# A gated recurrence with a convolution behind it: convolution sums in PSUM, q loaded one token to a partition, paired normalizers, and a new order of all steps

## The chip, the cores and the metric

The kernel runs on one core of a Trainium2 chip. The metric is the device time of one execution in microseconds (us). The core's engines are PE (matrix multiplication), DVE and ACT (elementwise work from SBUF or PSUM), POOL (elementwise work in SBUF), and SP, which here only issues DMAs. Every engine works through its own instructions in the order in which they were issued, and waits where one needs another engine's result.

## What is computed

Inputs are fp32: q, k, v, o_gate of shape (4, 8, 768, 40), i_gate and f_gate (4, 8, 768), w_val and w_out (320, 320), conv_w (5, 320).

```python
for t in range(S):                                   # mLSTM, per batch and head
    m_new  = max(f[t] + m, i[t])
    C = exp(f[t] + m - m_new) * C + exp(i[t] - m_new) * outer(v[t], k[t])
    n = exp(f[t] + m - m_new) * n + exp(i[t] - m_new) * k[t]
    y[t] = sigmoid(o[t]) * (C @ q[t]) / max(abs(n @ q[t]), 1)
x    = y as (B, S, H * D)                            # 320 columns
gate = sigmoid(sum_k conv_w[k] * x[t - 4 + k])       # causal, 5 taps
out  = (gate * (x @ w_val)) @ w_out
```

## The kernel before, in words

The sequence is cut into 6 tiles j of 128 tokens; tile j and batch b make unit u = 4j + b, and each unit's two halves of 64 tokens make the groups g = 2u + p, 48 in all. Within a group all 8 heads are worked at once in chunked form: a matrix of decays between the tokens of the half, a score matrix, and a carried state of 40 x 41 per head (the 41st column is n).

All work is a list of small steps in the string `PLAN`; a loop at the end calls each step's function in that order. `probs.7=V` runs probs for group 7 on DVE; V, A, P and S are DVE, ACT, POOL and SP's DMA queue. `args.2#5` is a PE step that writes PSUM bank 5. There are eight banks of 512 fp32 per partition. So the order on each engine is the order of its steps in `PLAN`, buffers are taken in rotation, and a step waits until its buffer or bank is free.

Steps that the change or the prediction speaks of, with their lines before:

- Loads: ldq (L404, L407) brings q. In tile 0 a partition holds one token; in later tiles the 128 partitions are four batches of 32, each with four tokens in a row (runs of 640 bytes). ldk, ldv, ldo bring k, v and the output gate; cpk (L416) copies k to the layout `kp` that the state needs, mostly as a DMA.
- Operands: mx and scs (L488, L502 to L507) find a power of two as scale for each token, hi (L534 to L538) and lo (L543) split q and k into fp16 parts in `stk`; then either a DMA transpose (trd, L555) or PE transposes and a copy out of PSUM (trp L560, trc L564) turn them.
- Since the scale of q lies four tokens to a partition, smul (L517), sout (L522) and sctc (L526) bring it to one token a partition by a small matmul.
- Group steps: args (L576, the exponents of the decays), expo (L580), scores (L593), probs (L598, score times decay into `pk`), keyw (L606, the weighted keys), then heads (L633, numerators and normalizer), state (L616, the carried state) or both in one (both, L642), and stout (L625, state back to SBUF).
- Unit steps: norm (L648 absolute value, L651 to L655 maximum with the scale, L657 reciprocal), rsm (L661, the output gate divided by the normalizer), gate (L664, x), xeh and xel (a split of x's last 64 columns), xtr (L686, PE transposes of x), xcc, xhc, x3c and xlo (the transposed x and its parts).
- Tile steps, the feed-forward part: cv0 (L722, the first tap, POOL) and cv (L728, four taps on DVE, each adding to `gt` in SBUF) for the first two column blocks of 128, cv3 (L748, L750, PE) for the third of 64, g3c, sigm (L761), val (L771), zmul (L776), zhi and zlo (a split), outp (L793), obc (L797), od (L800).
- Gate tables: sig_ and sia bring the gates' running sums into `la` and `ra`, the operands of args, one DMA for tile 0 and one for all other tiles; cla copies the constant part with a DMA of 600 KB.

Of the kernel before, what the change touches and what calls it, by code (L numbers as in the profile page):

```python
# [29 lines left out]
raj.1=A lo.0.0.0=V ldo.0=S scs.0.0.2.3.4.0=V mx.1.1.0=A trp.0.0.0#0 gates.1.7=V trp.0.1.1#1 trc.0.0.0=A  # L30
scs.0.0.2.1.2.3=V lo.0.1.0=V mx.0.2.0=A lo.0.0.1=V trp.0.1.0#2 scs.0.0.2.3.4.1=V trc.0.1.1=A trp.0.0.1#3
scs.0.0.2.3.4.3=V laj=V scs.0.0.2.2.3.0=V sia.0.0=S scs.0.0.2.0.1.3=V mx.1.0.0=A trc.0.1.0=V sig_.0=S mx.1.3.1=A
scs.0.0.2.2.3.1=V scs.0.0.2.2.3.3=V hi.0.2.1=P selb=V wcv.5.5=A wld.0.0=S wcv.5.3=V sia.0.1=A gates.1.8=V mx.1.1.1=A
ldv.0.0=S trc.0.0.1=V hi.0.3.0=A wld.1.0=S hi.0.2.0=V scores.1#4 mx.1.0.1=A gates.1.9=V sct0=A args.2#5 wcv.5.4=V
lo.0.2.1=V args.0#6 cpk.0.1.1=S scs.0.0.2.1.2.2=V trp.0.2.1#7 zcmp.1.1=V scs.0.0.2.0.1.2=V cpk.0.0.1=S sigo.0=A
wcv.0.0=V hi.0.3.1=V ldv.0.1=S scores.0#0 lo.0.3.0=V raj.3=V trp.0.3.0#1 wcv.0.1=V wcv.5.6=V scs.1.1.2.0.4.0=V
lo.0.2.0=V expo.0=A scs.1.1.2.0.4.1=V scs.1.0.1.0.4.0=V trp.0.2.0#2 lo.0.3.1=V wcv.0.5=A keyw.0=P args.1#3 probs.0=V
chh=A raj.5=A hi.1.0.1=V cdd.0.1=A both.0#6 expo.1=A wcv.0.2=V ldk.2.2.4=S scs.1.0.1.0.4.1=V gates.1.10=V trc.0.2.0=A
wcv.0.3=V ldq.2.0=S idk1.1=V trc.0.2.1=A args.4#0 wcv.0.4=P trp.0.3.1#3 probs.1=V wld.1.1=S args.7#2 idk0.1=A expo.2=A
args.3#7 wcv.0.6=V scores.3#4 ldk.2.0.2=S gates.1.11=V stout.0=A keyw.2=P scores.2#5 ldq.2.1=S hi.1.1.0=A heads.1#6  # L40
trc.0.3.1=V hi.1.0.0=A probs.2=V keyw.1=P hi.1.1.1=A lo.1.0.0=V both.2#3 soa.1.3=S whi.0.0=A scs.0.0.2.3.4.2=V
scs.0.0.2.2.3.2=V lo.1.1.0=V expo.3=A ldq.2.3=S norm.0.0=V lo.1.0.1=V state.1#5 wld.2.0=S stout.2=A norm.0.1=V
probs.3=V trc.0.3.0=A sog.1=S args.5#7 keyw.3=P wcv.1.0=V ldq.2.2=S args.6#4 expo.5=A trp.1.0.0#1 norm.0.2=V wld.2.1=S
wcv.1.1=V rsm.0=P expo.4=A scores.4#7 raj.4=V soa.1.2=S hi.1.2.0=A heads.3#3 keyw.4=P probs.4=V cpk.1.1.0=S expo.6=A
cdd.0.0=P gate.0=V cla.0=S scores.6#0 smul.1=P norm.1.0=A expo.7=A wcv.1.2=V wlo.0.0=P scores.7#7 norm.1.1=V
trc.1.0.0=V raj.2=A sout.1#4 soa.1.0=S trp.1.1.0#6 lo.1.1.1=V sctc.1=A mx.2.2.1=A zxc=P both.4#2 wcv.1.3=V sig_.1=S
trc.1.1.0=A norm.1.2=V wcv.1.4=P rsm.1=V soa.1.1=S mx.2.0.0=A trp.1.0.1#1 hi.1.3.0=P probs.6=V stout.4=A scores.5#4
cdd.0.4=A wcv.2.0=V xeh.0=P state.3#6 mx.2.0.1=A probs.5=V cdd.0.3=P cla.1=S open_late=X xel.0=P mx.2.2.0=A zx3=V
stout.1=V heads.5#2 mx.2.1.1=A keyw.6=V wcv.2.1=V mx.2.3.0=A both.6#0 lo.1.2.0=V wcv.2.5=A hi.1.2.1=V mx.2.1.0=A
scs.1.1.2.0.4.3=V trc.1.0.1=A gate.1=V trp.1.2.0#4 wcv.2.2=V trp.1.1.1#5 scs.2.0.1.0.4.0=V zcmp.1.0=V probs.7=V  # L50
stout.6=A xtr.0#3 sia.1.0=S scs.2.0.1.0.4.1=V norm.2.0=A keyw.5=V trc.1.2.0=A heads.7#0 cpk.1.0.0=S hi.1.3.1=V
ldv.1.0=S state.5#1 norm.2.1=V xeh.1=A lo.1.2.1=V mx.2.3.1=A lo.1.3.0=V norm.3.0=A stout.5=A norm.2.2=V trp.1.3.0#7
wcv.1.5=A rsm.2=P xhc.0=A trc.1.1.1=A trc.1.3.0=V ovc.1.0=P xel.1=P gate.2=V xtr.1#4 cdd.0.2=A sia.1.1=S wcv.2.3=V
args.10#1 x3c.1=A scs.2.1.2.0.4.0=V ldv.1.1=S scores.10#7 norm.3.1=V x3b.5=A scs.1.1.2.0.4.2=V stout.3=A wcv.1.6=V
# [892 lines left out]
```

## Time and profile before

| what | value |
|---|---|
| median of 3 runs | 249.64 us (248.62 to 251.87) |
| the profiled execution | 249.69 us |
| its span in the profile | 247.9 us |
| mean granted TensorE clock | 0.985 |
| DVE / PE / ACT / POOL busy | 221.7 / 210.1 / 171.3 / 119.6 us |

The profile is one execution. Its span runs from the first to the last instruction; the 1.8 us around it are launch and end. "Busy" counts an engine's instructions, not its waits. The ends of pipelined matmuls are modelled, so neighbouring PE rows overlap; from the start of one row to the start of the next is what it really took. A buffer's number is left out in the names, and `bank` stands for all eight PSUM banks.

### The profile page before, as it was taken

How to read it: one execution, taken by the hardware profiler on the slowest of the kernel's cores; microseconds unless marked ns; L12 is line 12 of the kernel's file. 1: busy time of each engine (PE TensorE's matmuls, PEld its weight loads, DVE VectorE, ACT ScalarE, POOL GpSimd, SP SyncE). 2: the span in 40 equal slices, each digit the busy share in tenths (PEclk: the TensorE clock that was granted, in tenths of full speed). 3: DMA queues.
4: the chain of work that ended last, by engine and by line, in shares of the span. 5: the costliest groups of instructions: out<-in, count | busy, mean ns of one | idle time of the engine just before them, and what ended most of it. 6: DMA issues, size and time to landing. Idle time of an engine off the chain costs nothing.

```text
span 247.9 us, 5992 instructions
## 1 busy us (share of the span) xinstructions
PE 210.1 (85%) x2141; PEld 180.4 (73%) x2141; DVE 221.7 (89%) x523; ACT 171.3 (69%) x395; POOL 119.6 (48%) x187
## 2 busy tenths in 40 slices
...
GB/s 137 151 121 157 154 154 202 201 168 146 150 150 193 155 170 170 176 222 161 175 171 189 216 195 184 169 208 162 140 95 149 71 71 1 0 82 54 79 108 106
DMA packets 130228, 35.72 MB, mean 144 GB/s; under 512 B 118310, under 2 KB 128086, under 8 KB 130198
## 3 DMA queue, kind: packets, MB, share of 16 engines
...
## 4 chain that ended last, share of the span: by engine, by line
PE 29%; DVE 26%; DMA 14%; ACT 10%; issue 8%; POOL 7%; SPq 3%; ACTq 0%; POOLq 0%; DVEq 0%
PE bank L642 7%; DMA sg<-in_o_gate_dram 5%; PE bank L633 5%; DVE sg L728 4%; PE bank L793 4%; DVE stk L543 3%; PE bank L771 3%; DMA out_dram<-ob 3%; ACT sg L761 2%; ACT junk L488 2%; DMA tq<-stk 2%; DVE pk L598 2%; DVE sg L776 2%; PE bank L593 2%; PE bank L560 2%
## 5 line engine op out<-in xcount | busy, mean ns | idle before, releaser
L642 PE MATMUL bank<-vc,pk 128*104 128x41 f32 x384 | 41.3, 270 | 1.7 <-DVE pk L606 1.0
L642 PEld LDWEIGHTS bank<-vc,pk 128*104 128x104 f32 x384 | 38.8, 178 | 3.8 <-DVE pk L606 1.1
L728 DVE SCALAR_TENSOR_TENSOR sg<-xc,cwt,sg 128x512 f32<-128x512 f32 (+1 forms) x56 | 40.2, 732 | 0.2
L598 DVE SCALAR_TENSOR_TENSOR pk<-bank,cmp,dm 128x512 f32<-128x512 f32 x48 | 35.4, 740 | 3.3 <-PE bank L593 2.4
L580 ACT ACTIVATE dm<-bank 128x512 f32<-128x512 f32 x48 | 28.3, 596 | 12.4 <-PE bank L576 5.0
L606 POOL TENSOR_TENSOR pk<-kp,dm 128x320 f32<-128x320 f32 (+1 forms) x27 | 22.8, 849 | 21.5 <-ACT dm L580 9.1
L593 PE MATMUL bank<-tq,tk 120*128 120x64 f16 x384 | 27.7, 243 | 5.8 <-DVE tk L564 3.2
L560 PE MATMUL bank<-idh,stk 128*120 128x128 f16 x128 | 13.7, 280 | 21.1 <-DVE stk L543 20.8
L593 PEld LDWEIGHTS <-tk 120*128 120x128 f16 x384 | 23.2, 122 | 11.3 <-issue 6.8
L633 PEld LDWEIGHTS bank<-vc,pk 104*64 104x64 f32 x384 | 24.6, 140 | 8.7 <-issue 2.7
L633 PE MATMUL bank<-vc,pk 104*64 104x41 f32 x384 | 27.4, 233 | 3.2 <-ACT vc L625 1.3
L543 DVE SCALAR_TENSOR_TENSOR stk<-nat,scl,stk 128x320 f16<-128x320 f32 x48 | 28.8, 605 | 1.5 <-POOL stk L538 1.3
L560 PEld LDWEIGHTS <-stk 128*120 128x120 f16 x128 | 12.5, 187 | 23.1 <-DVE stk L543 22.1
L534 ACT ACTIVATE stk<-nat,scl 128x640 f16<-128x640 f32 x27 | 21.8, 827 | 8.2 <-DVE scl L504 3.7
L661 POOL TENSOR_TENSOR rs<-sg,den 128x320 f32<-128x320 f32 x16 | 12.6, 788 | 29.6 <-DVE den L657 29.5
L488 ACT ACTIVATE junk<-nat 128x320 bf16<-128x320 f32 x48 | 22.5, 469 | 4.7 <-DMA nat<-in_q_dram 3.0
L625 ACT COPY vc<-bank 40x328 f32<-40x328 f32 x36 | 15.3, 424 | 13.1 <-PE bank L642 10.9
L793 PE MATMUL bank<-woh,zh 128*128 128x320 f32 x72 | 19.6, 328 | 0.5 <-DVE x L707 0.4
L711 POOL TENSOR_TENSOR xl<-xc,xh 128x256 fp32r<-128x256 f32 x18 | 15.3, 853 | 8.5 <-ACT xh L699 6.3
L576 PE MATMUL bank<-ra,la 120*128 120x512 bf16 x48 | 19.3, 427 | 0.0
L793 PE MATMUL bank<-wol,zh 128*128 128x320 f32 x72 | 18.3, 309 | 0.0
L538 POOL TENSOR_SCALAR stk<-nat,scl 128x640 f16<-128x640 f32 x10 | 8.8, 882 | 19.7 <-ACT junk L488 9.5
...
## 6 DMA issues: line engine op xcount, KB each, us to landing
nat<-in_q_dram SPq DMA_DIRECT2D x24, 160.0 KB, 3.9
...
vc<-in_v_dram SPq DMA_DIRECT2D x12, 320.0 KB, 6.5
out_dram<-ob SPq DMA_DIRECT2D x24, 160.0 KB, 1.8
kp<-nat SPq DMA_DIRECT2D x22, 160.0 KB, 3.1
nat<-in_k_dram SPq DMA_DIRECT2D x10, 320.0 KB
...
raw<-in_moe_w_val_dram SPq DMA_DIRECT2D x5, 160.0 KB, 3.1
```

The source lines that it names most:

```text
L488: A.activation(junk, part(j, x, i), AF.Abs, accum_out=amx[j % 2][:, x, i : i + 1])
L534: A.activation(o, s, AF.Copy, scale=f)
L543: V.scalar_tensor_tensor(t[:, :, c : c + D], part(j, x, i), scl[j % 2][:, x, i : i + 1], t[:, :, 0:D], op0=ALU.mult, op1=ALU.subtract,)
L560: nc.tensor.transpose(t[0:K3, h], stk[(j * B + i) % NSTK][:, x, h, 0:K3], id16)
L580: A.activation(dms[g % NDM], late["psd", g], AF.Exp)
L593: nc.tensor.matmul(o, tk[h], tq[:, h], start=True, stop=True)
L598: V.scalar_tensor_tensor(pks[g % NPK][:, :, 0:L], late["pss", g], cmp_[j % 2][:, p, b : b + 1], dms[g % NDM], op0=ALU.mult, op1=ALU.mult,)
L606: eng[e].tensor_mul(pks[g % NPK][0:n, :, L:], kp[0:n, p, b * H : (b + 1) * H], dms[g % NDM][0:n, :, L - 1 : L].to_broadcast([n, H, D]),)
L633: nc.tensor.matmul(ph[p * L : (p + 1) * L, h], pks[g % NPK][0:n, h, 0:L], vc[j % 2][0:n, p, b * H + h], start=True, stop=True,)
L642: nc.tensor.matmul(ph[0 : L + D, h], pks[g % NPK][:, h], vc[j % 2][:, p, b * H + h], start=True, stop=True)
L728: V.scalar_tensor_tensor(o, xc[j % 2][:, c, b0:b1, t : t + P], cwt[:, c, t : t + 1], o, op0=ALU.mult, op1=ALU.add)
L793: nc.tensor.matmul(po, z, w, start=(i == 0), stop=(i == len(mm) - 1))
```

## The change

The functions change as follows (helpers that are no longer called are left out):

```diff
-    NTK, NTQ, NSTK, NDM, NPK, NX, NRS, NOB, NDEN, NXE = 3, 2, 2, 3, 2, 2, 2, 2, 3, 2
+    NTK, NTQ, NSTK, NDM, NPK, NX, NRS, NOB, NDEN, NXE = 3, 2, 3, 3, 3, 3, 3, 2, 3, 3
+    SL = 2
-    la = cst.tile([KA, 2, NJ, B, P], BF16, name="la")
+    la = cst.tile([KA, 2, SL, B, P], BF16, name="la")
...
     def ldq(e, j, b):
...
-        if j == 0:
-            hs = slice(b * H, (b + 1) * H)
-            dma(e)(nat[0][:, 0, hs], qv[ts, hs])
-            return
-        dst = nat[j % 2][:, 0].rearrange("p (h r) d -> p h (r d)", r=R)
-        dma(e)(dst[b * PB : (b + 1) * PB], q[b, :, ts].rearrange("h (g r) d -> g h (r d)", r=R))
+        hs = slice(b * H, (b + 1) * H)
+        dma(e)(nat[j % 2][:, 0, hs], qv[ts, hs])
...
+    def sig_(e, j):
+        src = gdg[min(j, 1)].rearrange("x p b h j t -> (x p b) h j t")
+        dma(e)(ra[L : L + NGR, :, j % SL], src[:, :, max(j - 1, 0)])
...
+    def warm(b_, i):
+        for _ in range(8):
+            nc.tensor.matmul(bank(b_, H, L), tl[:, 0, 0], tr, start=True, stop=True)
...
     def norm(e, u, s):
...
-        elif s == 0:
-            V.tensor_scalar(d, nq, -1.0, sct[j % 2][:, b : b + 1], op0=ALU.mult, op1=ALU.max)
-        elif s == 1 and ("na", u) in late:
-            V.tensor_scalar_max(d, d, sct[j % 2][:, b : b + 1])
+        d = dens[u // 2 % NDEN]
+        if s == 0:
+            A.activation(d[:, u % 2], late["ph", u][:, :, D:DT], AF.Abs)
         elif s == 1:
-            V.tensor_tensor(d, nq, d, op=ALU.max)
+            c = scl[j % 2][:, 0, b : b + 2, None, None].to_broadcast([P, 2, H, 1])
+            eng[e].tensor_tensor(d, d, c, op=ALU.max)
...
-            xi = xf[:, c * P : (c + 1) * P] if c < 2 else xes[u % NXE].bitcast(F32)
-            nc.tensor.transpose(px[:, c], xi, ident)
+            if c < 2:
+                nc.tensor.transpose(px[:, c], xf[:, c * P : (c + 1) * P], ident)
+            else:
+                nc.tensor.transpose(px[:, c].bitcast(F32R), xes[u % NXE], idr)
```

`PLAN` is new from the first step to the last. One line of its convolution, before and now:

```diff
-norm.5.2=V trd.2.2.0=S wcv.3.0=V keyw.15=P probs.15=V args.20#6 keyw.16=P stout.14=V sigo.1=A ldv.2.0=S whi.2.3=V
-heads.15#3 cv0.0.1.0.4=P norm.4.2=V ldv.2.1=S hi.2.2.1=A state.15#5 rsm.5=V rsm.4=V stout.13=A cpk.2.1.0=S lo.2.2.1=V
+expo.36=A probs.35=V heads.33#4 stout.34=A gate.14=V state.33#3 cva.2.0.0.4#2 lo.4.3.1=V heads.34#6 x3c.13=A keyw.35=V
+trd.4.3.1=S expo.37=A keyw.36=P cvp.2.0.1.0.4=V cva.2.1.0.4#5 state.35#7 cpk.4.1.1=P cvp.2.0.2.0.4=V heads.35#6
```

In counts of steps, before and after:

| step | before | after |
|---|---|---|
| first tap | 14 cv0 on POOL | 14 cva on ACT, into a PSUM bank |
| taps 2 to 5 | 56 cv on DVE, sums in SBUF | 56 cvp on DVE, sums in the bank, the fifth tap's result to SBUF |
| norm on DVE | 24 + 10 + 24, one unit each | 12 + 12, two units each |
| norm on ACT (absolute value) | 14 | 24 |
| smul / sout / sctc / selb, selg, sct0 | 5 / 5 / 5 / 3 | none |
| both / heads / state | 24 / 24 / 20 | 0 / 48 / 44 |
| cpk | 22 DMAs, 2 DVE | 2 DMAs, 2 DVE, 9 ACT, 11 POOL |
| cla / sig_ / sia | 2 / 2 / 4 DMAs | 0 / 6 / 12, each tile's own |
| warm (8 args-shaped matmuls, result unused) | 0 | 3 |
| hi: DVE, ACT, POOL | 11, 27, 10 | 5, 24, 19 |
| keyw: DVE, POOL | 17, 27 | 10, 34 |
| rsm: DVE, POOL | 8, 16 | 4, 20 |
| trc: DVE, ACT | 5, 11 | 10, 6 |
| xlo: DVE, POOL | 6, 18 | 11, 13 |
| zhi: DVE, ACT | 4, 17 | 10, 11 |
| scs (scales of q and k): DVE | 46 | 36 |

On DVE, the first column block's convolution of tile 0 before: `sg` holds the sums, and the taps (L728) stand between a state copy (L625), probs (L598), the low parts of the operands (L543) and single normalizers (L653, L657).

```order
L625 COPY vc1_82<-bank0_68 40x328
L543 SCALAR_TENSOR_TENSOR stk1_113<-nat0_78,scl0_108,stk1_113 128x8x40
L728 SCALAR_TENSOR_TENSOR sg_83<-xc0_86,cwt_95,sg_83 128x512
L598 SCALAR_TENSOR_TENSOR pk0_118<-bank7_75,cmp1_102,dm2_117 128x8x64
L543 SCALAR_TENSOR_TENSOR stk0_112<-nat0_78,scl0_108,stk0_112 128x8x40
L728 SCALAR_TENSOR_TENSOR sg_83<-xc0_86,cwt_95,sg_83 128x512
L653 TENSOR_SCALAR den1_121<-den1_121,sct1_104 128x8
L657 RECIPROCAL den2_122<-den2_122 128x8
L829 TENSOR_SCALAR wa_151<-raw1_148 128x320
L598 SCALAR_TENSOR_TENSOR pk1_119<-bank5_73,cmp1_102,dm0_115 128x8x64
```

Now, on DVE at tile 0's convolution; the first rows are the second column block's sum in bank 2, `bank5` is the first block's, L622 is the step gate, L613 a paired maximum.

```order
L700 SCALAR_TENSOR_TENSOR bank2_70<-xc0_87,cwt_96,bank2_70 128x512
L663 COPY xc1_88<-bank3_71 128x2x128
L700 SCALAR_TENSOR_TENSOR bank2_70<-xc0_87,cwt_96,bank2_70 128x512
L480 TENSOR_SCALAR amx1_107<-amx1_107 128x8
L482 TENSOR_SCALAR scl1_105<-amx1_107 128x8
L622 TENSOR_TENSOR x1_125<-bank5_73,rs1_122 128x320
L700 SCALAR_TENSOR_TENSOR bank2_70<-xc0_87,cwt_96,bank2_70 128x512
L506 SCALAR_TENSOR_TENSOR stk1_109<-nat1_80,scl1_105,stk1_109 128x8x40
L700 SCALAR_TENSOR_TENSOR bank5_73<-xc0_87,cwt_96,bank5_73 128x512
L613 TENSOR_TENSOR den1_119<-den1_119,scl0_104 128x16
L700 SCALAR_TENSOR_TENSOR sg_84<-xc0_87,cwt_96,bank2_70 128x512
```

The sum of a block moved from SBUF to a bank until its last tap, the taps of the two blocks stand among each other, and the normalizer's row has 16 columns.

On PE in tile 0 before: scores of group 5 (L593), state of group 3 (L616), heads of group 5 (L633), the fused step of group 6 (L642), then transposes for tile 1 (L560).

```order
L593 LDWEIGHTS tk2_98
L593 MATMUL bank4_72<-tq0_99,tk2_98 128x64
L616 MATMUL bank6_74<-vc0_81,pk1_119 40x41 x8
L633 MATMUL bank2_70<-vc0_81,pk1_119 64x41 x8
L642 MATMUL bank0_68<-vc0_81,pk0_118 104x41 x8
L560 LDWEIGHTS stk0_112
L560 MATMUL bank4_72<-idh_77,stk0_112 120x128
```

Now, on PE in tile 1, heads (L595) and state (L578) of groups 11 to 14, with an args matmul (L543) between.

```order
L595 MATMUL bank0_68<-vc1_83,pk2_117 64x41 x8
L578 MATMUL bank2_70<-vc1_83,pk2_117 40x41 x8
L595 MATMUL bank1_69<-vc1_83,pk0_115 64x41 x8
L543 LDWEIGHTS la_85
L543 MATMUL bank7_75<-ra_86,la_85 128x512
L578 MATMUL bank4_72<-vc1_83,pk0_115 40x41 x8
L578 MATMUL bank2_70<-vc1_83,pk2_117 40x41 x8
L595 MATMUL bank5_73<-vc1_83,pk2_117 64x41 x8
L578 MATMUL bank4_72<-vc1_83,pk1_116 40x41 x8
L595 MATMUL bank1_69<-vc1_83,pk1_116 64x41 x8
```

The fused step is gone; heads and state of a group follow one another or stand some steps apart, each writing a bank of its own.

## Rows read from the trace of the kernel before

**Rows 1.** The profile's page: busy time, share of the span and instructions of each engine; and, from its fourth part, the chain of work that ended last, by engine.

```profile
PE 210.1 (85%) x2141; PEld 180.4 (73%) x2141; DVE 221.7 (89%) x523; ACT 171.3 (69%) x395; POOL 119.6 (48%) x187
...
PE 29%; DVE 26%; DMA 14%; ACT 10%; issue 8%; POOL 7%; SPq 3%; ACTq 0%; POOLq 0%; DVEq 0%
```

**Rows 2.** Busy time of each engine in five stretches of the span. [...]

```profile
0.00:20.00 20.00, 0.00 (x0) 0.00 (x0) 16.69 (x43) 10.66 (x22) 11.61 (x31) 1.00 0.86 135
20.00:57.80 37.80, 32.09 (x356) 28.20 (x356) 34.54 (x92) 33.91 (x80) 13.25 (x19) 0.95 0.96 173
57.80:181.40 123.60, 114.90 (x1254) 96.19 (x1251) 114.47 (x269) 96.75 (x221) 66.66 (x99) 0.99 1.18 175
181.40:226.40 45.00, 44.95 (x403) 38.44 (x403) 40.07 (x89) 20.96 (x51) 22.09 (x30) 1.00 0.33 67
226.40:247.90 21.50, 18.14 (x135) 17.55 (x133) 15.95 (x34) 9.02 (x23) 5.97 (x9) 0.99 0.25 85
```

**Rows 3.** The timeline of PE, its last row. Columns: start us, us, engine, line, operation, out<-in, shapes, count.

```profile
244.23 0.31 PE L793 MATMUL bank<-wol,zh 128*128 128x320 f32 x1
```

**Rows 4.** The timeline of PE at places where it works without a gap (L576 args, L593 scores, L633 heads, L616 state, L642 the fused step, L686 transposes of x, L771 val). Columns as above; `[idle before <-releaser]` at a row's end where PE waited.

```profile
76.37 0.81 PE L616 MATMUL bank<-vc,pk 104*40 104x41 f32 x16
77.12 0.62 PE L593 MATMUL bank<-tq,tk 120*128 120x64 f16 x8
...
193.81 1.13 PE L633 MATMUL bank<-vc,pk 104*64 104x41 f32 x16
194.87 1.66 PE L642 MATMUL bank<-vc,pk 128*104 128x41 f32 x16
196.35 0.39 PE L576 MATMUL bank<-ra,la 120*128 120x512 bf16 x1
196.58 0.38 PE L686 MATMUL bank<-ident,x 128*128 128x128 f32 x2
...
198.29 1.52 PE L593 MATMUL bank<-tq,tk 120*128 120x64 f16 x24
199.62 0.83 PE L576 MATMUL bank<-ra,la 120*128 120x512 bf16 x2
200.38 0.95 PE L633 MATMUL bank<-vc,pk 104*64 104x41 f32 x13
...
201.84 1.66 PE L642 MATMUL bank<-vc,pk 128*104 128x41 f32 x16
...
203.61 0.71 PE L771 MATMUL bank<-xh,wvh 128*128 128x512 f32 x2
...
205.55 0.45 PE L793 MATMUL bank<-woh,zh 128*128 128x320 f32 x2
```

**Rows 5.** Groups of PE instructions by line from 57.8 to 181.4 us. Columns: line, engine, operation, out<-in, shapes, count | busy us, mean ns of one | idle time before them and what ended it.

```profile
L642 PE MATMUL bank<-vc,pk 128*104 128x41 f32 x256 | 26.3, 263 | 1.7 <-DVE pk L606 1.0 <-DVE x L664 0.3 <-ACT den L648 0.2
L593 PE MATMUL bank<-tq,tk 120*128 120x64 f16 x248 | 19.0, 249 | 2.2 <-DMA tk<-stk 1.5 <-DVE pk L598 0.4 <-ACT tk L564 0.4
L633 PE MATMUL bank<-vc,pk 104*64 104x41 f32 x240 | 17.2, 234 | 2.2 <-ACT vc L625 1.3 <-DVE vc L625 0.8
L576 PE MATMUL bank<-ra,la 120*128 120x512 bf16 x34 | 13.0, 400 | 0.0
L616 PE MATMUL bank<-vc,pk 104*40 104x41 f32 x243 | 12.9, 208 | 0.9 <-DVE pk L598 0.5 <-DVE den L657 0.4
```

**Rows 6.** Groups of DVE instructions by line and shape, whole span. Columns as in the group above.

```profile
L598 DVE SCALAR_TENSOR_TENSOR pk<-bank,cmp,dm 128x512 f32<-128x512 f32 x48 | 35.4, 740 | 3.3 <-PE bank L593 2.4 <-PE bank L642 0.4 <-ACT dm L580 0.4
L728 DVE SCALAR_TENSOR_TENSOR sg<-xc,cwt,sg 128x512 f32<-128x512 f32 x40 | 32.0, 807 | 0.1
...
L776 DVE TENSOR_TENSOR sg<-bank,sg 128x512 f32<-128x512 f32 x10 | 6.8, 685 | 0.8 <-PE bank L771 0.7
...
L657 DVE RECIPROCAL den<-den 128x8 f32<-128x8 f32 x24 | 4.7, 197 | 0.3
L699 DVE CAST xh<-bank 128x256 fp32r<-128x256 f32 x11 | 4.6, 415 | 0.1
L661 DVE TENSOR_TENSOR rs<-sg,den 128x320 f32<-128x320 f32 x8 | 3.9, 500 | 0.2
...
L653 DVE TENSOR_SCALAR den<-den,sct 128x8 f32<-128x8 f32 x14 | 3.9, 276 | 0.7 <-ACT den L648 0.7
...
L858 DVE CAST wvh<-wf 128x256 fp32r<-128x256 f32 x1 | 0.3, 278 | 0.0
```

**Rows 7.** The instructions of two lines, probs (L598) and the convolution taps (L728). Columns: line, engine, operation, names, count: shortest/median/longest in ns, first and last start in us; shapes.

```profile
L598 DVE SCALAR_TENSOR_TENSOR pk<-bank,cmp,dm x48: 692/740/753, 32.3 to 213.9; 128x512 f32<-128x512 f32 x48
...
L728 DVE SCALAR_TENSOR_TENSOR sg<-xc,cwt,sg x56: 469/743/1284, 77.9 to 238.3; 128x512 f32<-128x512 f32 x40, 128x256 f32<-128x256 f32 x16
```

**Rows 8.** DMA: the packets of the span by size; and the issues by out<-in, with queue, operation, count, KB of each, median us from issue to landing.

```profile
DMA packets 130228, 35.72 MB, mean 144 GB/s; under 512 B 118310, under 2 KB 128086, under 8 KB 130198
...
nat<-in_q_dram SPq DMA_DIRECT2D x24, 160.0 KB, 3.9
...
vc<-in_v_dram SPq DMA_DIRECT2D x12, 320.0 KB, 6.5
```

**Rows 9.** Groups of instructions from the page's fifth part: the exp on ACT and the subtraction xlo on POOL.

```profile
L580 ACT ACTIVATE dm<-bank 128x512 f32<-128x512 f32 x48 | 28.3, 596 | 12.4 <-PE bank L576 5.0
...
L711 POOL TENSOR_TENSOR xl<-xc,xh 128x256 fp32r<-128x256 f32 x18 | 15.3, 853 | 8.5 <-ACT xh L699 6.3
```

More of the change, by code (lines that the diff above doesn't have):

```diff
@@ L30 @@
[L30 to L54, printed above, removed]
```

337 lines of the change are left out of this document (161 added, 176 removed).

## The prediction

> **What bounds the kernel now.** I read the page's busy line first: DVE 89%, PE 85%, ACT 69%, POOL 48%, and a chain that changes engine all the time (PE 29%, DVE 26%, DMA 14%) [rows 1]. An average of two engines near 90% decides nothing, so next come the busy times by stage, cut where the program changes character [rows 2]. Until 57.8 us (last heads matmuls of tile 0) the program fills: PE does not start before 20 us, DVE is busy 16.7 of 20.0 and then 34.5 of 37.8 us. From 57.8 to 181.4 us tiles overlap: PE 114.9 and DVE 114.5 of 123.6 us. From 181.4 to 226.4 us PE is full (44.95 of 45.0). The rest is the tail; the last matmul ends at 244.5 us, 3.4 us before the span's end [rows 3]. So three limits follow one another: DVE with its feeders at the start, a tie in the middle, PE alone at the end. DVE time saved at the end is worth nothing.
>
> How much PE loses in the middle is read from dense pitches, start to start, since modelled ends overlap [rows 4]: an args matmul 0.23 us (196.35 to 196.58), eight scores 0.44 (1.33 for 24), heads and state side by side 1.46 (200.38 to 201.84), the fused step 1.49 (194.87 to 196.35), a val step of eight 1.94. Times the counts of that stage ([rows 5], 16 records a step for heads, state and the fused one, 8 for scores): fused 16 x 1.49 = 23.8; heads with state 15 x 1.46 = 22, up to 27 where they stand apart (heads alone 1.06, from 193.81 to 194.87, state alone 0.75, from 76.37 to 77.12); scores 31 x 0.44 = 13.6; args 34 x 0.23 = 7.8; from the order, nine val steps (66 matmuls) x 0.24 = 16; eight outp of eight matmuls of 320 columns, 5/8 of val's, x 1.2 = 9.7; three third-block convolutions of ten matmuls x 0.24 = 7.2; transposes about 6. Together 106 to 111, say 108. Of 123.6 us, 15.6 are lost: 8.7 shown idle, about 1.2 from the granted clock of 0.99, the rest as stretched records. That is all a faster DVE can give back in the middle.
>
> **The change part by part.** Durations are those of the profiled execution: 249.69 us, a span of 247.9 and 1.8 around it; the median of the runs is 249.64, so no correction.
>
> *DVE* [rows 6]. Normalizers: before 14 x 276 and 24 x 197 ns, and 20 more rows of about 0.19 = 12.3 us; after 12 maxima and 12 reciprocals of 16 columns. No row has 16 columns: from the same as for 8 (197) to double; at 200 each, 4.8 us: -7.5. Key and query scales of eight columns instead of twice four: ten rows fewer of that small size, at 0.23: -2.3. Selection helpers gone, five at most 0.3: about -1.3. To other engines: hi 6, keyw 7, rsm 4; from them: trc 5, xlo 5, zhi 6. All are of 250 to 1000 columns and near the row of rs, 0.5: 17 x 0.5 out, 16 x 0.5 in, -0.5. Small casts, fills, weight splits and gate steps: some fifteen rows fewer at about 0.5: -8.
>
> *Convolution.* All 56 taps stay on DVE, now from and into a PSUM bank; POOL's first tap becomes 14 ACT copies. No row has the new form. The nearest is the probs product, same instruction, 128x512, one operand from PSUM, 740 ns, with 692 to 753 over 48 [rows 6, 7], while the taps take 807 at that size and scatter from 469 to 1284 [rows 7]. Taken at 740: 56 x 67 ns = -3.8. Lower bound: zmul, a product with PSUM of that size, 685, gives 56 x 122 = -7. Upper: a cast that reads PSUM takes 415 against 278 from SBUF; if the 42 taps that write PSUM paid these 137 ns for it, +5.8, less the 3.8, is +2.
>
> [...]
>
> The sum for DVE is -23.4 us of rows. Neighbouring records overlap (all groups of that view add up to some 253 us against 221.7 busy), so about -20 of busy time: 221.7 to some 201.
>
> *ACT and POOL* [rows 9]. ACT: +14 copies for the first taps and +9 key copies, all near the 0.6 of an exp, and +10 small absolute values, against three hi, five trc (about 1.0 each) and six zhi: +14.8 less 11, +4 on 171.3. POOL: +11 key copies, +9 hi, +7 keyw, +4 rsm, less 14 first taps, five xlo, four scale products: 8 rows net, at the 0.85 of an xlo row +7 on 119.6, and to +17 with fills, gate and weight steps put there: 52 to 56% of the span. Both are hidden as long as a key copy is done before its tile's first keyw, else each costs its own 0.6 to 0.9 us in front of a state step: POOL is busy 66.7 of 123.6 us in the middle, ACT 96.8 [rows 2].
>
> *DMA.* Twenty copies of keys (160 KB each) and two copies of tables leave the queue. q in 160-byte runs instead of 640 adds packets; those of tile 0 go that way already, and v, in the same runs, lands in 6.5 us for 320 KB, against 3.9 for q's 160 KB [rows 8]: q lands 0 to 2.6 us later. It is issued a tile ahead: no cost. [...] The gate tables refilled by tile (sig_, sia) wait on SP until the tile two before has done its last args; behind them stand operand transposes and output stores. I cost that at nothing, since each refill stands a tile ahead of its use; if it is wrong, scores wait for the transposes, some us a tile, which is case (a).
>
> *PE.* Heads alone take 1.06, state alone 0.75, the two side by side 1.46, so 0.35 is saved where they are neighbours that write different halves of the partitions. Before: 24 x 1.49 + 24 x 1.06 + 20 x 0.75, less 16 such neighbours x 0.35 = 70.6. After: 48 x 1.06 + 44 x 0.75 - 41 x 0.35 = 69.5. So -1, and +13 if none of them saved anything, which the row of 200.38 excludes for most. Five scale matmuls go: -0.3. The warm packs are 24 matmuls of the args shape at 0.23 to twice that at half the clock: +5.5 to +11. The first pack stands in PE's waits at the start, the other two (3.7 to 7.4) after the eleventh and twelfth args, in tile 1: with the savings +4 in the middle. They may lift the clock of the start (0.95 until 57.8 us [rows 2], about 1.9 us lost); not counted.
>
> **The sum along the path.** Start: DVE steps up to the eighth probs shrink by about 5 us (in rows: hi -2, gates -3, norm -3, gate -2, trc +3), but ACT's list up to the eighth exp grows by as much; I take half: 57.8 - 3 = 54.8. Middle: 108 work + 4 added + 8 of the 15.6 lost, since DVE's 20 us of relief and a third buffer for probs, x and stacked operands remove waits on DVE but not those on DMA and clock = 120. End: 63.1 from 181.4 to 244.5, PE-full, unchanged, and 3.4. Together 241.3 of span, + 1.8 = 243.1 us.
>
> **The rivals.** (a) Nothing gained in the middle: PE work is the bound, the lost 15.6 us come from the order (waits on transposes and evictions) and come back elsewhere. For it: in the rows of the middle no releaser of PE has more than 1.5 us, and DVE is only one of them [rows 5]. 54.8 + 123.6 + 4 + 66.5 = 248.9 of span, 250.7 us. (b) Slower: the sums hold banks. Each of 14 sums sits in one of eight banks from ACT's copy to the fourth tap; four taps at 0.74 with other DVE rows between them are 5 to 6 us, two at a time in places, and PE, in order, stands before any matmul planned for that bank. It decides once a hold delays PE by 0.8 us on average (14 x 0.8 over 243.1 passes 254.6): at 1 us each it is 257 us. For it: in the order PE has only one to five steps between the place of the last tap and the next matmul into that bank, never more than two sums at once. Against it: the last tap goes to SBUF and ends the hold, and at a PE step of 0.4 to 2 us two steps cover a tap that is two places late. (c) Much faster: PE loses 5 in the middle and the start follows DVE entirely: 51.8 + 113 + 66.5 = 231.3, 233 us. (d) Dear taps: writing a bank costs what reading one costs a cast, the upper bound above; DVE saves 15 instead of 20, the start regains 2 and the middle 6: 55.8 + 122 + 66.5 + 1.8 = 246 us.
>
> **How the numbers follow.** About 2% (244.6 and 254.6 us) is what a measurement of this kernel can tell from no change. Forecast 0.42, (c) and steps towards it 0.1, (d) 0.13, (a) 0.22, (b) 0.13. Faster by over 2%: most of the forecast and (c), together 0.50; slower: (b) and the far side of (a), 0.16; within: 0.34. Range 232 to 255: from (c) through (a), the far part of (b) left out. The likeliest alone: 239 to 247.
>
> **What would show it.** Right: the tap row in PSUM near 740 ns with a narrow spread; normalizer rows of some 200 ns, 24 in all; DVE busy near 201 us; PE's stage from tile 1 to the fifth tile's first heads shorter by about 4 us and as full as now in the last 60; POOL below 60%. Wrong: taps above 800 ns (d); PE idle with a convolution tap as releaser (b); PE idle in the middle traced to POOL's keyw or key copies; or heads and state, apart, taking over 1.6 together in the full stretches.

## The result

The changed kernel took 234.65 us (median of 4 runs, 231.87 to 242.1) against 250.75 us for the kernel before on the same chips (248.62 to 253.71): a ratio of 0.931, 95% interval 0.914 to 0.949 (the ratio is that of each kernel's fast executions, within 1.5% of its fastest; the two medians give 0.936). Forecast were 243.1 us, a range of 232 to 255, and 0.50 for faster. The direction was right and the time lies in the range, but the gain is about two and a half times the forecast one.

One thing is needed to read every number below: executions of the same kernel differ by stretches of 3 to 27 us in which PE's granted clock is 0.5 of the full one, and so a time means little without the mean clock beside it. The profile taken with the result had such stretches:

```profile
PEclk9999999558999959589999999999999999999999
```

Its mean clock was 0.943 and it took 242.1 us; eight transposes of `stk` took 0.88 us in it at half clock (46.26 to 47.14) and 0.45 at the full one (58.95 to 59.40). The other three executions had 0.978 to 0.984 and 231.87 to 235.36 us. So the lines below are from a second profile of the same kernel, 229.73 us at 0.993 (run e1_after). Its page:

```profile
span 227.9 us, 6769 instructions
...
PE 196.6 (86%) x2544; PEld 168.5 (74%) x2544; DVE 204.1 (90%) x448; ACT 177.6 (78%) x413; POOL 127.6 (56%) x216
...
PEclk9999999999999889999999999999999999999999
```

Against [rows 1]: DVE 204.1 us (forecast 201), PE 196.6 (before 210.1), POOL 56% (forecast 52 to 56). The stages, cut at the same places in the work as [rows 2], the third at the scores of group 40, which stand at 182.3 us before and at 162.9 now. The columns, here and in [rows 2]: stretch, its length, busy us and (instructions) of PE, PE's weight loads, DVE, ACT and POOL, the granted clock (1.00 is the full one), the mean DMA share, GB/s.

```profile
0.00:20.00 20.00, 2.22 (x16) 1.83 (x16) 17.98 (x44) 17.72 (x40) 11.04 (x32) 1.00 0.93 148
20.00:50.00 30.00, 26.41 (x411) 22.60 (x412) 29.16 (x64) 27.48 (x63) 18.77 (x30) 1.00 0.95 154
50.00:162.90 112.90, 107.88 (x1534) 90.06 (x1533) 103.12 (x217) 101.14 (x236) 77.75 (x127) 0.98 1.14 168
162.90:205.00 42.10, 40.80 (x456) 35.73 (x453) 37.76 (x88) 22.30 (x56) 15.18 (x24) 1.00 0.41 77
205.00:227.90 22.90, 19.31 (x139) 18.33 (x137) 16.09 (x40) 8.99 (x21) 4.85 (x5) 1.00 0.19 65
```

Start 57.8 to 50.0 us (-7.8, forecast -3); middle 124.5 to 112.9 (-11.6, forecast -3.6); end 65.6 to 65.0 (forecast 0). PE in the middle is busy 107.9 us with 5.0 idle, where it was 115.8 and 8.7 up to the same scores. So two thirds of what the middle gained is work that PE no longer does, and that term was not in my sum. (That PE has less to do is not enough by itself: see f1.)

DVE's rows by shape, which answer to [rows 6, 7]:

```profile
L560 DVE SCALAR_TENSOR_TENSOR pk<-bank,cmp,dm 128x512 f32<-128x512 f32 x48 | 34.8, 738 | 4.6 <-PE bank L555 3.1 <-PE bank L595 1.0 <-ACT dm L547 0.3
...
L700 DVE SCALAR_TENSOR_TENSOR bank<-xc,cwt,bank 128x512 f32<-128x512 f32 x30 | 22.0, 740 | 0.3
...
L700 DVE SCALAR_TENSOR_TENSOR sg<-xc,cwt,bank 128x512 f32<-128x512 f32 x10 | 7.4, 738 | 0.1
...
L700 DVE SCALAR_TENSOR_TENSOR bank<-xc,cwt,bank 128x256 f32<-128x256 f32 x12 | 5.5, 482 | 0.0
...
L615 DVE RECIPROCAL den<-den 128x16 f32<-128x16 f32 x12 | 2.9, 242 | 0.1
...
L613 DVE TENSOR_TENSOR den<-den,scl 128x16 f32<-128x16 f32 x12 | 2.3, 190 | 0.1
```

The tap in a bank takes 740 and 738 ns, as taken, and 482 for 256 columns; 24 normalizer rows of 242 and 190 ns make 5.2 us (4.8 taken).

### The profile page after: what moved, and what is told of

Its sections match the earlier page's. It is cut to its first block, busy times and chain, and to the rows that moved or that the text cites. A ratio compares the mean times of both kernels' runs of the same rounds, so it can differ in the third digit from the quotient of the medians.

```text
span 240.3 us, 6769 instructions
## 1 busy us (share of the span) xinstructions
PE 207.4 (86%) x2544; PEld 177.7 (74%) x2544; DVE 205.2 (85%) x448; ACT 178.1 (74%) x413; POOL 126.5 (53%) x216
## 4 chain that ended last, share of the span: by engine, by line
PE 55%; DVE 18%; DMA 9%; ACT 6%; SPq 5%; issue 4%; POOL 2%; DVEq 0%; POOLq 0%; ACTq 0%
PE bank L595 14%; PE bank L731 9%; PE bank L753 8%; PE bank L578 7%; DMA tq<-stk 4%; PE bank L543 4%; PE bank L555 4%; PE bank L710 3%; DMA raw<-in_moe_w_val_dram 3%; DVE pk L560 3%; DVE bank L700 3%; PE bank L523 2%; DVE stk L506 2%; DVE sg L736 1%; PE bank L533 1%
## 5 line engine op out<-in xcount | busy, mean ns | idle before, releaser
L595 PE MATMUL bank<-vc,pk 128*64 128x41 f32 (+1 forms) x768 | 58.7, 242 | 3.4 <-DVE pk L560 3.3
L595 PEld LDWEIGHTS bank<-vc,pk 128*64 128x64 f32 (+1 forms) x768 | 53.6, 150 | 8.9 <-DVE pk L560 4.3
L560 DVE SCALAR_TENSOR_TENSOR pk<-bank,cmp,dm 128x512 f32<-128x512 f32 x48 | 34.7, 735 | 9.1 <-PE bank L555 5.7
L578 PE MATMUL bank<-vc,pk 128*40 128x41 f32 (+1 forms) x704 | 37.6, 211 | 0.3 <-POOL pk L568 0.3
L578 PEld LDWEIGHTS bank<-vc,pk 128*40 128x40 f32 (+1 forms) x704 | 32.7, 125 | 2.6 <-issue 1.5
L568 POOL TENSOR_TENSOR pk<-kp,dm 128x320 f32<-128x320 f32 (+1 forms) x34 | 25.5, 756 | 14.4 <-ACT dm L547 6.0
L700 DVE SCALAR_TENSOR_TENSOR bank<-xc,cwt,bank 128x512 f32<-128x512 f32 (+1 forms) x42 | 27.4, 666 | 0.5 <-ACT bank L694 0.3
L501 POOL TENSOR_SCALAR stk<-nat,scl 128x640 f16<-128x640 f32 x19 | 17.0, 898 | 11.4 <-DVE scl L482 8.2
L555 PEld LDWEIGHTS <-tk 120*128 120x128 f16 x384 | 15.7, 102 | 5.9 <-issue 3.6
L555 PE MATMUL bank<-tq,tk 120*128 120x64 f16 x384 | 18.4, 199 | 1.5 <-DMA tq<-stk 1.4
L543 PE MATMUL bank<-ra,la 120*128 120x512 bf16 x48 | 18.2, 418 | 0.2 <-DVE sg L736 0.2
L745 POOL TENSOR_TENSOR zl<-sg,zh 128x512 fp32r<-128x512 f32 (+1 forms) x5 | 5.6, 1124 | 19.6 <-ACT vc L587 8.4
```

Source lines behind the costliest of these rows:

```text
L543: nc.tensor.matmul(psd, la[:, p, j % SL, b], ra[:, :, j % SL], start=True, stop=True)
L555: nc.tensor.matmul(pss[:, h], tk[h], tq[:, h], start=True, stop=True)
L560: V.scalar_tensor_tensor(pks[g % NPK][:, :, 0:L], late["pss", g], cmp_[j % 2][:, p, b : b + 1], dms[g % NDM], op0=ALU.mult, op1=ALU.mult,)
L568: eng[e].tensor_mul(pks[g % NPK][0:n, :, L:], kp[0:n, p, b * H : (b + 1) * H], dms[g % NDM][0:n, :, L - 1 : L].to_broadcast([n, H, D]),)
L578: nc.tensor.matmul(pc[n0 : n0 + D, h], pks[g % NPK][0:n, h, L:], vc[j % 2][0:n, p, b * H + h], start=True, stop=True)
L595: nc.tensor.matmul(ph[p * L : (p + 1) * L, h], pks[g % NPK][0:n, h, 0:L], vc[j % 2][0:n, p, b * H + h], start=True, stop=True,)
```

## The experiments

Each is one edit, timed beside the kernel before in three series (e, f, g) on three chips. Times are medians of at least four executions, with the range of the mean clock. The kernel before took 246.98, 246.92 and 246.75 us in the three series at clocks of 0.978 and 0.979, so times of different series can be set side by side. At one and the same clock executions of one kernel still differ by 2 us and more (231.87 and 233.93 us at 0.984 and 0.982), so a difference between single pairs is good to about that.

**e1_after and e3_no_warm.** The changed kernel again, and without its three packs of unused matmuls:

```diff
-... warm.2#5 ... warm.1#4 ... warm.0#0
```

> The changed kernel once more, unedited, for a profile at the full clock: the one at hand has a granted clock of 0.943, with half-clock stretches between 40 and 60 and between 80 and 104 us. Expected 231 to 235 us. If the gain comes from waits removed in the middle (my sum: 8 of 15.6 us kept, middle stage 120), probs of group 8 starts within 3 us of before (62.1 us) and the gain grows steadily to probs of group 40; if it comes from the start, probs of group 8 is already 8 us or more early; if from the end, the time from the last probs to the end is shorter by 5 us or more (34 us before).

> The three packs of eight unused matmuls left out. My sum charged 4 us of PE time to them in tile 1: if PE's work sets the time there, 3 to 5 us faster. Rival: the packs hold up the granted clock, or fill waits that are there anyway: without them the same time within 1 us at an unchanged clock, or up to 5 us slower with a mean clock lower by 0.01 to 0.03.

Measured: 233.73 us (229.73 to 236.63, clock 0.971 to 0.993) and 231.0 us (228.71 to 236.83, 0.942 to 0.992). PE is busy 4.8 us less without the packs (196.6 to 191.8), and the two executions at 0.993 and 0.992 differ by 1.0 us, those at 0.984 and 0.982 by 2.8 (233.56 and 230.81): of the 4 us charged 1 to 3 were paid, and these runs don't fix it closer. Both kernels have executions with few and with many half-clock stretches; what the packs do for the clock these runs don't show. In e1 the probs of group 8 start at 55.9 us instead of 62.1, so in this pair a third of the gain comes from the start. It hangs on the clock: in the profile at 0.943, at half clock from about 42 to 56 us, they start at 62.6.

**e4_two_buffers and e2_sums_sbuf.**

```diff
-    NTK, NTQ, NSTK, NDM, NPK, NX, NRS, NOB, NDEN, NXE = 3, 2, 3, 3, 3, 3, 3, 2, 3, 3
+    NTK, NTQ, NSTK, NDM, NPK, NX, NRS, NOB, NDEN, NXE = 3, 2, 2, 3, 2, 2, 2, 2, 3, 2
```

and in e2, besides:

```diff
+    cs = cst.tile([P, 2, B, P], F32, name="cs")
-        pv = bank(b_, b1 - b0, P)
+        pv = cs[:, c, b0:b1]
```

> The changed kernel with two buffers again, instead of three, for the stacked operands, probs, x, the gate over normalizer, and the split of x. If the order of the steps needs the third buffers: 4 to 10 us slower, with new waits of DVE or ACT for PE on these tiles. Rival (the order, and less work on DVE, make the gain): within 2 us of the changed kernel.

> Two buffers as in the run that has only that (see e4_two_buffers, with which it is to be compared), and the convolution sums in an SBUF tile of their own instead of PSUM banks; ACT still makes the first tap, DVE the other four. Theory (the tap reading and writing a bank is cheaper): taps back to about 807 ns and a wide spread, DVE busy +3 to +4 us, time +1 to +4 us against e4. Rival (the sums hold banks that PE waits for): time 2 to 5 us below e4. [...]

Measured: 255.83 us (0.924 to 0.931) and 264.17 us (0.921 to 0.954). In this order, with two buffers, steps overwrite a tile before an earlier group has read it (in `PLAN`, for 19 groups, probs or keyw of the group two later stands before the step that reads the `pk` it overwrites), so in both kernels part of the products are of other data, and the 255.83 us don't price the third buffers. The two kernels compare with each other: SBUF sums cost 8.3 us, against the expected 1 to 4, and the taps became 919 ns on average instead of 741. That is tested with three buffers in f3.

**f1_before_q.** The kernel before with its own order and only the layout of q changed. The diff is the one of `ldq`, `part` and `scores` in the change; the scales of q are copied where they were brought by a matmul, and smul, sout, selb and selg go.

> The kernel before, with its own order, and one part of the change alone: q one token to a partition in all tiles, so that the scores read their moving operand in one run of 64 tokens and write the bank in order, and the scale matmuls with their DVE and POOL helpers go. The trace of before has the scores of tile 0, whose q lies so already, at 0.23 us for eight (45.97 to 46.20), and 0.43 in the later tiles; 40 groups x 0.20 = 8 us of PE work that my sum left out. Theory (that was the missing term): eight scores take 0.23 in all tiles, PE busy 8 to 10 us less, time 6 to 10 us less (about 240 to 244). Rival (DVE bounds this order in the middle): the pitch falls, but PE waits instead, time within 3 us of before.

The expectation rests on two rows of the kernel before that I had not read in this light. Tile 0's scores:

```profile
45.97 0.39 PE L593 MATMUL bank<-tq,tk 120*128 120x64 f16 x8 [0.33 <-DVE pk L598]
46.20 0.17 PE L522 MATMUL bank<-sel_b,spg 128*128 128x4 bf16 x1
```

Eight in 0.23 us, against 0.44 in [rows 4]. Measured: the pitch did fall to 0.23 or 0.24 in all tiles, but the kernel took 253.97 us (253.36 to 256.87, clock 0.918 to 0.958), where the kernel before took 251.96 (246.92 to 259.52, 0.906 to 0.979) in the same series: 2 us more, within the 3 of the rival. At like clocks no gain stands out either: 253.78 us at 0.958 stands against 251.79 to 252.65 at 0.958 and 0.959, and 253.36 at 0.929 against 255.73 at 0.926. The stages of its profile, and of the kernel before, with the granted clock as the column before the DMA share:

```profile
20.00:38.00 18.00, 13.86 (x134) 11.15 (x134) 16.68 (x47) 17.76 (x39) 4.21 (x5) 1.00 1.02 162
38.00:66.00 28.00, 27.61 (x245) 25.40 (x246) 17.31 (x51) 19.43 (x50) 7.81 (x16) 0.52 1.05 172
66.00:84.00 18.00, 16.02 (x230) 13.65 (x228) 17.80 (x43) 14.67 (x40) 9.43 (x14) 0.99 0.75 120
```

```profile
20.00:38.00 18.00, 13.88 (x102) 11.42 (x103) 17.00 (x48) 17.68 (x40) 3.96 (x5) 1.00 0.99 159
38.00:66.00 28.00, 25.27 (x348) 22.64 (x347) 24.98 (x69) 24.06 (x59) 11.46 (x19) 0.94 0.99 182
```

After a wait at 38.4 us the clock of f1 is at half (0.52) through the next 28 us, where before it is 0.94, and DVE starves (25.0 to 17.3 us busy). Its profile, at 0.918 over 255 us, ran some 41 us at half speed. That lengthens this execution, but does not tell where the saved work went. The stretch from the 29th probs to the last shows that, with the clock at 1.00 in both kernels, before and in f1:

```profile
134.20:213.90 79.70, 77.31 (x788) 65.54 (x787) 72.77 (x165) 50.80 (x110) 39.07 (x57) 1.00 0.82 134
```

```profile
141.60:220.60 79.00, 73.82 (x785) 62.11 (x784) 73.14 (x164) 51.10 (x111) 38.94 (x56) 1.00 0.85 136
```

PE is busy 3.5 us less, and the stretch is shorter by 0.7: PE waits instead, as the rival had it. So in the old order the layout alone is worth 0.7 us in this stretch, and nothing that can be seen over the whole. What holds this order there is not shown: DVE is busy 73 of 79 us in both, but no single releaser stands out in PE's waits.

**f2_strided.** The other way round: the changed kernel with scores in interleaved quarters.

```diff
-            nc.tensor.matmul(pss[:, h], tk[h], tq[:, h], start=True, stop=True)
+            o, m = (t.rearrange("k (g r) -> k r g", r=4) for t in (pss[:, h], tq[:, h]))
+            nc.tensor.matmul(o, tk[h], m, start=True, stop=True)
```

> The changed kernel, with the scores' 64 columns taken and written in four interleaved quarters, as the kernel before did in tiles 1 to 5 (every fourth token), though all of one batch, so that no step waits for anything new. The result is the same. Theory (pitch): eight scores 0.43 instead of 0.23, PE work +9 to +10 us, time +6 to +10 us. Rival (the gain of the layout is that a batch's scores no longer wait for all four transposes of a tile): pitch up, time within 3 us.

Its scores, eight from 104.29 to 104.75, and those of e1, sixteen in 0.47:

```profile
104.29 0.64 PE L556 MATMUL bank<-tq,tk 120*128 120x64 f16 x8
104.75 0.40 PE L543 MATMUL bank<-ra,la 120*128 120x512 bf16 x1
```

```profile
62.44 0.64 PE L555 MATMUL bank<-tq,tk 120*128 120x64 f16 x16
62.91 0.38 PE L543 MATMUL bank<-ra,la 120*128 120x512 bf16 x1
```

Measured: 235.99 us (235.21 to 236.7), PE busy +8.3 us. Beside e1's execution at 0.993 that is +6.3 us, the low end of the theory's 6 to 10; beside e1's median it is only +2.3, because here the clock stayed at 0.998 to 1.000 in all four executions (that the fuller PE is the reason is not shown). Beside g4 below, which ran at 0.993 to 1.000 too, it is +4.3. So it is 4 to 6 us.

No new wait was added here, so in the new order the pitch itself carries this, not the wait for a tile's four transposes.

**f3_sums_sbuf.** Three buffers, 13 of 14 sums in SBUF.

```diff
-        pv = bank(b_, b1 - b0, P)
+        pv = ...   # a tile of 2 KB a partition (c = 0), or one of the weights' raw tiles, free by then (c = 1, j > 0)
```

> The changed kernel with three buffers kept and 13 of the 14 convolution sums in SBUF tiles of their own instead of PSUM banks (the second block of tile 0 stays in its bank). In the pair of runs with two buffers the 512-column tap took 919 ns in SBUF, 471 to 2255, against 741 in a bank, 475 to 757. Theory (a tap with two SBUF inputs is held up while POOL works, one with a bank input is not): taps again 850 to 950 on average with the same shortest ones as in a bank, DVE busy +8 to +12, POOL's own instructions longer too, time +5 to +10 us. Rival (that difference came with the two buffers' other waits): taps at 740 to 800, time within 2 us.

Measured: 242.28 us (241.25 to 245.51, clock 0.963 to 0.977). At like clocks 241.25 at 0.977 stands against 235.36 at 0.978, and 242.05 at 0.971 against 236.63 at 0.971: +5.4 to +5.9 us. (One tile serves a whole column block, so the first tap of tile 5's second block writes `raw`, at 213.39 us, before the last two taps of tile 4's have read it: part of those gate sums are of other data, here and in g1. It made DVE wait 0.25 us.) The taps by where their sum lies, the last row being the one sum left in a bank; then shortest, median and longest in SBUF, and in a bank in e1:

```profile
L706 DVE SCALAR_TENSOR_TENSOR cs<-xc,cwt,cs 128x512 f32<-128x512 f32 x15 | 14.3, 956 | 0.9 <-ACT cs L700 0.6
...
L706 DVE SCALAR_TENSOR_TENSOR raw<-xc,cwt,raw 128x512 f32<-128x512 f32 x12 | 10.7, 888 | 0.3 <-ACT raw L700 0.2
...
L706 DVE SCALAR_TENSOR_TENSOR bank<-xc,cwt,bank 128x512 f32<-128x512 f32 x3 | 2.2, 746 | 0.0
```

```profile
L706 DVE SCALAR_TENSOR_TENSOR cs<-xc,cwt,cs x21: 473/749/1653, 91.9 to 230.5; 128x512 f32<-128x512 f32 x15, 128x256 f32<-128x256 f32 x6
```

```profile
L700 DVE SCALAR_TENSOR_TENSOR bank<-xc,cwt,bank x42: 473/743/756, 85.0 to 214.9; 128x512 f32<-128x512 f32 x30, 128x256 f32<-128x256 f32 x12
```

The shortest tap is the same (473), the median nearly (749 and 743); the mean is not, because some taps take up to 1653 ns. These are taps that overlap a POOL instruction: of the 36 taps of 512 columns in SBUF, the six that overlap none take 661 to 754 ns, the other thirty up to 1653, 955 on average; in a bank, in e1, the 31 that overlap one take 668 to 756. The same three taps of tile 4, with POOL at work, here and in e1:

```profile
202.87 3.93 DVE L706 SCALAR_TENSOR_TENSOR cs<-xc,cwt,cs 128x512 f32<-128x512 f32 x3
```

```profile
192.42 2.33 DVE L700 SCALAR_TENSOR_TENSOR bank<-xc,cwt,bank 128x512 f32<-128x512 f32 x3
```

POOL's rs and xlo suffer with them, here and in e1:

```profile
L620 POOL TENSOR_TENSOR rs<-sg,den 128x320 f32<-128x320 f32 x20 | 17.4, 874 | 12.7 <-DVE den L616 8.7 <-ACT junk L470 3.9
...
L672 POOL TENSOR_TENSOR xl<-xc,xh 128x256 fp32r<-128x256 f32 x13 | 13.1, 1012 | 0.2
```

```profile
L619 POOL TENSOR_TENSOR rs<-sg,den 128x320 f32<-128x320 f32 x20 | 14.9, 752 | 11.1 <-DVE den L615 7.1 <-ACT junk L469 4.0
...
L671 POOL TENSOR_TENSOR xl<-xc,xh 128x256 fp32r<-128x256 f32 x13 | 10.3, 799 | 0.2
```

DVE is busy 14.4 us more (218.5), POOL 12.4 more (140.0). The theory holds as far as these rows go: with both inputs in SBUF a tap takes up to 1653 ns beside POOL, and POOL's xlo 1012 ns instead of 799; with its sum in a bank a tap takes 668 to 756 beside POOL.

**f4_norm_single.** Each paired maximum and reciprocal as two of 8 columns.

```diff
-            c = scl[j % 2][:, 0, b : b + 2, None, None].to_broadcast([P, 2, H, 1])
-            eng[e].tensor_tensor(d, d, c, op=ALU.max)
+            for i in range(2):
+                V.tensor_scalar_max(d[:, i], d[:, i], scl[j % 2][:, 0, b + i : b + i + 1])
```

> The changed kernel with the maxima and reciprocals of a pair as two instructions of 8 columns each, at the places of the paired ones: 24 DVE instructions more. The rows of before have 276 and 197 ns for these, the changed kernel 243 for a reciprocal of 16: DVE rows +4 to +5 us. If DVE is what the middle waits for: +2 to +4 us. If PE is: within 1 us.

Measured: 233.72 us (231.58 to 243.19, 0.941 to 0.985); that it is e1's median to the hundredth is chance. The two profiles at 0.943 (243.19 and 242.1 us) have their half-clock stretches at the same places, and DVE busy 208.2 and 205.2 us. So 3 us of DVE rows cost about 1 us in the new order.

**g1_strided_sbuf.** The edits of f2 and f3 together.

> The changed kernel with both suspects undone: scores in four interleaved quarters, and 13 of 14 convolution sums in SBUF. Alone the first gave 236.0 us at a granted clock of 0.998 to 1.000, the second 242.3 at 0.963 to 0.977, against 233.7 at 0.971 to 0.993 unedited. Theory (these two parts are most of the gain): the losses add, 8 + 6 to 9 us over the 229 us of full clock, 243 to 247 us at a clock above 0.98, near the kernel before. Rival (both are paid on the same waits, and the rest of the gain is the order's): 236 to 241 us.

Measured: 243.41 us (243.03 to 244.19, clock 0.990 to 0.992), +13.3 us on e1's 229.73 at 0.993, or +11.7 on g4's median at 0.993 to 1.000; the two alone were +4.3 to +6.3 and about +5.7. They add, as the theory had it, and together are most of the difference to the kernel before, whose executions at 0.978 and 0.979 took 246.75 to 249.85 us.

**g2_keys_dma.** The key copies of tiles 1 to 5 as DMAs.

```diff
-cpk.3.0.0=P ... cpk.4.1.1=P ...
+cpk.3.0.0=S ... cpk.4.1.1=S ...
```

> The changed kernel with the key copies of tiles 1 to 5 (16 of 20, those on ACT and POOL) as DMAs on SP's queue again, at the same places. My sum costed these copies at nothing as long as ACT and POOL cover them. Theory (covered): time within 2 us, ACT and POOL busy 12 us less together. Rival (POOL in order is loaded, the copies delay keyw): 2 to 4 us faster. Rival (a key copy by DMA waits behind others on SP's queue and holds keyw): 2 to 6 us slower, POOL or DVE waiting for kp from a DMA.

Measured: 242.7 us (0.963 to 0.969), +5.6 in the one pair at like clock (242.25 at 0.969, 236.63 at 0.971), +9.0 by the medians. The second rival was right. Two rows of the waits (engine, line, releaser: us, times, longest) say why:

```profile
POOL pk L568 <- DMA kp<-nat: 17.5, 6, 5.2
...
DVE pk L568 <- DMA kp<-nat: 4.2, 2, 3.7
```

**g3_fused.** Heads and state fused in 18 of 24 first halves.

```diff
-... heads.2#4 ... state.2#0 ...
+... both.2#4 ...
```

> The changed kernel with heads and state of 18 of the 24 first halves fused again into one step of 104 output rows, at the later of their two places before the second half's heads. My sum: PE work equal, 1.49 against 1.46 and 0.35 more where they stand apart. Theory (apart matters only for PE's time): within 2 us. Rival (apart, the state needs the weighted keys alone and not probs, so the carried state of the next half is ready earlier): 2 to 6 us slower, PE or the state copy waiting.

Measured: 237.28 us (236.26 to 242.05), at 0.920 to 0.956. Inconclusive: the clock was low in every execution, and at 0.942 it took 237.6 us where the unfused kernel took 242.1 at 0.943. The median is 3.6 us above e1's. Whether fusing costs anything apart from the clock, or brings the low clock about, these runs don't show.

**g4_fill.** Packs of four unused matmuls where PE waits, in place of two of the packs of eight.

```diff
-... warm.1#4 ... warm.0#0
+... fill.0#0 trp.1.1.0#0 ... fill.1#2 trp.1.3.1#2 ... fill.1#7 xtr.2#7
```

> The changed kernel with the two packs of unused matmuls of tile 1 left out and three packs of four put where PE waits in the trace of the run at 0.993: before the transposes at 39 us (0.86 us idle), at 56.6 us (1.38) and before x's transposes at 76 us (1.66). Theory (the runs differ by stretches at the half clock that begin after such waits): granted clock 0.99 or more in every run, 228 to 231 us, with little spread. Rival (the falls have another cause): clocks from 0.94 to 0.99 as now, 230 to 242 us.

Measured: 231.74 us (230.9 to 232.39), clock 0.993 to 1.000 in all four:

```profile
PEclk9999999999999999999999999999999999999999
```

The clock is as expected, the time 0.7 us above the expected range. Its median is 2 us below e1's and its spread 1.5 us instead of 7; the best single execution, 228.71 us, is e3's, whose worst is 236.83. The two were timed in different series, so that g4 beats the changed kernel on average is likely and not shown. Nor is it shown that the place of the packs is the reason: f2 held 0.998 to 1.000 with the three packs of eight where they were.

## Why the prediction was right, and where it was wrong

*Right.* The direction; the durations: taps 740 in a bank, normalizers, POOL and DVE totals; and -3.5 us of tap rows (40.3 to 36.8) where -3.8 was taken. My -67 ns is not a property of the tap itself: the shortest taps are equal in f3 and e1 (473 ns) and the medians within 6 ns (749 and 743). What the rows show is that the long taps stand beside POOL: in f3 up to 1653 ns there, 661 to 754 without.

*Luck: that the time lies in the range.* The lower end, 232, is rival (c), and its middle of 113 us is 108 of work and 5 lost, without the 4 that the forecast adds for the packs. With them (c) is 237 us, and a range from there would have missed 234.65. So the gain was larger than any of the cases foresaw.

*Rival (b), held banks,* did not come. PE's waits in e1:

```profile
PE bank L523 <- DVE stk L506: 19.9, 5, 14.6
PE bank L595 <- DVE pk L560: 1.9, 4, 0.8
PE bank L644 <- DVE pk L560: 1.7, 1, 1.7
PE bank L555 <- DMA tq<-stk: 1.6, 2, 1.3
PE bank L523 <- ACT tq L527: 1.4, 1, 1.4
```

None is for a tap (L700). The first is the fill at the start: 14.6 us of it stand before PE's first matmul.

*Wrong: "108 work" in the middle, taken as unchanged.* I priced the removed scale matmuls and the split of heads and state (1.47 for a pair by itself in e1, from 35.82 to 37.29 us, as taken), but not that scores become cheaper when their columns lie in one run. 33 groups of the middle x (0.43 - 0.23) = 6.6 us of the 7.9 us that PE is busy less there, and f2 prices it at 4 to 6 us on the whole. The row was in the trace that I had. But f1 adds a condition that the sum would have needed too: in the old order the same work, taken off PE, became waits of PE. It turned into time only together with the rest of the change; with which part of it is not shown.

*Wrong: the start, half of DVE's 5 us.* It gained 7.8 in this pair of profiles. About 1.9 is the clock, 1.00 now from 20 to 50 us where it was 0.95 [rows 2]. That column does not show all of it: up to 39 us the kernel before takes 0.43 us for each args matmul (37.21 to 38.06 for two), e1 0.22 at 28 us already, though the column reads 1.00 for both:

```profile
37.21 1.06 PE L576 MATMUL bank<-ra,la 120*128 120x512 bf16 x2
38.06 1.06 PE L593 MATMUL bank<-tq,tk 120*128 120x64 f16 x16
```

```profile
28.03 0.38 PE L543 MATMUL bank<-ra,la 120*128 120x512 bf16 x1
28.25 1.89 PE L533 MATMUL bank<-tr,tl 120*128 120x512 bf16 x8
```

So PE came to its full pace about 12 us earlier. How the 7.8 us divide between this and DVE's shorter list is not shown, and so neither is whether ACT's longer list took back its half.

*Wrong in size: what the convolution's sums in banks are worth.* The rows promised -3.8 us; undone inside the new order they cost 5.4 to 5.9 us of time and 14 us of DVE rows. I took the scatter of the taps before (469 to 1284 ns) as given, and the trace of before shows what it is: of its 40 taps of 512 columns, the 20 that overlap no POOL instruction take 701 to 752 ns, the other 20 up to 1284, 873 on average. The longest, and POOL at that time:

```profile
212.66 1.28 DVE L728 SCALAR_TENSOR_TENSOR sg<-xc,cwt,sg 128x512 f32<-128x512 f32 x1
...
212.67 0.72 POOL L661 TENSOR_TENSOR rs<-sg,den 128x320 f32<-128x320 f32 x1 [2.29 <-DVE den L657]
213.38 1.13 POOL L722 TENSOR_SCALAR sg<-xc,cwt 128x512 f32<-128x512 f32 x1
```

The kernel before had POOL busy 48%, now it is 56%, with hi, keyw and key copies moved to it; f3 prices taps in SBUF beside that load.

*Not borne out: "DVE time saved at the end is worth nothing".* From the last probs to the end f2 takes 36.1 us, g1, which differs only in the sums, 40.5, with DVE busy 4.7 us more. So most of what the sums cost stands in the stage that I had called PE-full:

```profile
197.30:233.40 36.10, 32.72 (x241) 30.20 (x237) 28.40 (x70) 14.74 (x36) 10.37 (x12) 0.99 0.16 55
```

```profile
200.70:241.20 40.50, 33.32 (x241) 30.25 (x238) 33.12 (x70) 14.68 (x36) 12.18 (x12) 0.98 0.14 49
```

*Not borne out in size: DVE's relief as such.* f4 gives 3 us of it back at a price of about 1. It says this of the new order only; the old one was not tested so. *Costed at nothing, rightly on the engines:* the key copies; but I did not see that the DMA form would cost 5.6 us in this order, POOL waiting 17.5 us for `kp`, which has one buffer.

*Left open:* how the remainder divides between the order, third buffers and the table refills; which part of the change lets PE's saved work count; what the packs do to the clock; and whether it is the strided read or the strided write that makes eight scores 0.46 instead of 0.23.
